# Start-up of a Fourier-mixing and gated feed-forward kernel: 128-row first stage, new transfer order, rounding on GpSimd, weight folding ahead of the activation

## The chip, the cores and the metric

One core of a Trainium2 chip. The metric is device time in microseconds (us) for one execution. Every run is compared with runs of the kernel before on the same chip in the same rounds. A ratio is the mean time of one kernel's fast runs over the mean time of the other's fast runs of the same rounds, so it is not quite the ratio of the medians that are quoted beside it.

## The reference

```python
def _attn_ref(x):                       # x: 8 x 3008 x 256, float32
    X = np.fft.fft(x, axis=1)
    X = np.fft.fft(X, axis=2)
    return X.real.astype(np.float32)

def _moe_ref(x, w_in, w_out):           # 24064 x 256, 256 x 2048, 2048 x 256
    h = x @ w_in
    g = h * (1.0 / (1.0 + np.exp(-1.702 * h)))
    return (g @ w_out).astype(np.float32)
```

## The kernel before

A sequence of 3008 is split as 94 x 32. Stage 1 is a matmul over 94 rows for each of 32 columns (folded to 16 by symmetry). A shuffle brings its result to 128 partitions, and stage 2 finishes the transform along the sequence. The transform along the 256 features is folded into the input weights (`fold_w`). Then come 384 steps of hidden layer, activation and output product. The weights arrive as 64-bit words and are rounded to float32 on the chip in eight blocks. Only the start-up differs between the two kernels: stage 1 of batch 0, the shuffle, the rounding and the weight folding of steps 1, 3 and 5.

```python
def fold_first(c):                      # a quarter of batch 0: 94-row sums and differences
    t = xt[0]
    el, eu = (hp.tile([NA, 4, D], F32, tag="h", name=n) for n in ("el", "eu"))   # NA = 94; hp has 4 buffers
    ...                                 # two small ScalarE copies and four VectorE operations a quarter; three and six in the first
def mix_first(c):
    ...
            nc.tensor.matmul(ps[:, o + c0:o + c1], lhsT=mat(w1, l0, 128), rhs=el[:, q, c0:c1], start=True, stop=False)
            nc.tensor.matmul(ps[:, o + c0:o + c1], lhsT=upper, rhs=eu[:, 3 - q, c0:c1], start=False, stop=True)

def bounds(key):                        # first half of the rounding of one weight block
    nc.scalar.activation(g[:], hi, ACTF.Square)
    nc.gpsimd.tensor_scalar(m[:], hi, scalar1=TOP, scalar2=-TOP, op0=ALU.min, op1=ALU.max)
    nc.scalar.activation(r[:].bitcast(F32), lo, ACTF.Copy, scale=2.0 ** -29, bias=2.0 ** 23)   # low word
    nc.scalar.activation(r[:], r[:].bitcast(F32), ACTF.Copy, bias=-2.0 ** 23)                   # low word
def rounded(out, key):                  # second half: three VectorE passes, then one GpSimd addition
    ...
def round_in(n):
    wst[n] = hp.tile([128, 2, 512], F32, tag="h", name="wst")
    ...
    # start of the program, cut
    warm(8); bounds(("in", 0)); round_in(0); finish_in(0)
    for c in range(4):
        fold_first(c)
        if c:
            mix_first(2 * c - 2); mix_first(2 * c - 1)
    mix_first(6); mix_first(7)
    shuffle_first(nc.sync, 0, 1); shuffle_first(nc.scalar, 2, 3); shuffle_first(nc.sync, *range(4, NG))
    load_in(2, nc.sync); fold_w(0)
    bounds(("in", 1)); round_in(1); finish_in(1)
    load_out(1, nc.sync); nyquist_weights(0); rotate(0, 0, 4, nc.scalar.copy)
    ...
    at(1, fold_w, 1); at(1, nyquist_weights, 1); at(1, rotate, 0, 4, NG)      # and 3, 5 with blocks 2, 3
    for t in range(n + LAG):
        hidden(t); product(t - LAG); activate(t); combine(t - LAG)           # bounds of t cut
        for fn, args in extra.get(t, ()): fn(*args)                          # the at(...) work
```

Of the kernel before, what the change touches and what calls it, by code (L numbers as in the profile page):

```python
# [24 lines left out]
F32 = mybir.dt.float32  # L25
# [20 lines left out]
def free(ap, offset, *dims):  # L46
    return bass.AP(ap.tensor, ap.offset + offset, [list(ap.ap[0])] + [list(d) for d in dims])


def tables(S, D):  # L50

    assert S == NA * NB and D == 256
    H = D // 2
    a, u = np.arange(NG)[:, None], np.arange(NU)[None, :]
    ks = (NG * u + a).reshape(-1)
    s = NB * np.arange(NA)[:, None, None] + np.arange(NB)[None, :, None]
    angle = 2.0 * np.pi * ((s * ks) % S) / S
    cos, sin = np.cos(angle), np.sin(angle)
    w1 = np.zeros((NA, NW + NX, NG * NU, 2))
    w1[:, 1:16, :, 0], w1[:, 1:16, :, 1] = cos[:, 1:16], sin[:, 1:16]  # L60
    w1[:, 0, :, 0], w1[:, 16, :, 1] = cos[:, 0], cos[:, 16]
    w1[:, 17, :, 0], w1[:, 18, :, 1] = sin[:, 0], sin[:, 16]
    w1[:, NW:, :, 0], w1[:, NW:, :, 1] = cos[:, :16:-1], -sin[:, :16:-1]

    j, k2 = np.arange(16)[:, None], np.arange(NB)[None, :]
    beta = 2.0 * np.pi * ((j * k2) % NB) / NB
    m2 = np.zeros((NU, 2, 16, 2, NU, NB))
    rot = np.zeros((NU, 2, 16, NU, 2, 16))
    ends = np.stack([np.ones(NB), 1.0 - 2.0 * (np.arange(NB) % 2)])
    for i in range(NU):  # L70
        m2[i, 0, :, 0, i], m2[i, 1, :, 0, i] = np.cos(beta), -np.sin(beta)
        m2[i, 0, :, 1, i], m2[i, 1, :, 1, i] = np.sin(beta), np.cos(beta)
        m2[i, :, 0, 0, i] = m2[i, :, 0, 1, i] = ends
        for n in range(16):
            rot[i, 0, n, i, 1, n], rot[i, 1, n, i, 0, n] = (1.0, -1.0) if n else (0.0, 0.0)
        rot[i, 0, 0, i, 0, 0] = rot[i, 1, 0, i, 1, 0] = 1.0

    m, d = np.arange(D)[:, None], np.arange(H)[None, :]
    phi = 2.0 * np.pi * ((m * d) % D) / D
    cd = np.stack([np.cos(phi), -np.sin(phi)], 1)  # L80
    cd[:, 1, 0] = 1.0 - 2.0 * (np.arange(D) % 2)
    cd = cd.reshape(2, H, 2, H).transpose(1, 0, 2, 3)
    small = [t.reshape(128, -1) for t in (m2, rot, cd)]
    return w1.reshape(NA, NW + NX, 96).astype(np.float32), np.concatenate(small, 1).astype(np.float32)


@with_exitstack
def kernel(ctx: ExitStack, tc, x, w_in, w_out, tab1, tab2, out):
# [20 lines left out]
    Xr = [nc.dram_tensor(f"Xr{b}", (NA, 15, D), F32, kind="Internal").ap() for b in range(B)]  # L109
    Td = [nc.dram_tensor(f"Td{b}", (NG * 128, D), F32, kind="Internal").ap() for b in range(B)]  # L110

    w1 = const.tile([NA, NW * 96 + 32], F32, tag="w1", name="w1")
    small = const.tile([128, 2 * 128 + 128 + 4 * H], F32, tag="small", name="small")
    m2 = small[:, 0:256].rearrange("p (c n) -> p c n", c=2)
    rot = small[:, 256:384]
# [5 lines left out]
    af2 = const.tile([128, NF], F32, tag="af2", name="af2")  # L121
    ones = const.tile([1, 128], F32, tag="ones", name="ones")

    def mat(w, j, n=96):
        return w[:, j * 96:j * 96 + n]

    def bank(name):
        return psm.tile([128, 512], F32, tag="mm", name=name)
# [64 lines left out]
    e4 = {}  # L193

    def load_first(c):
        t, src = xt[0], x[0].rearrange("(p j) d -> p j d", j=NB)
        for lo, hi in (((0, 4), (29, 32), (16, 17)), ((4, 8), (25, 29)), ((8, 12), (21, 25)), ((12, 16), (17, 21)))[c]:
            for p0, p1 in PIECES:
                nc.sync.dma_start(out=t[p0:p1, lo:hi, :], in_=src[p0:p1, lo:hi, :])

    def fold_first(c):

        t = xt[0]
        el, eu = (hp.tile([NA, 4, D], F32, tag="h", name=n) for n in ("el", "eu"))
        e4[c] = el, eu
        first = 29 - 4 * c
        runs = [(el, 0, 4 * c, 4, False)]
        runs += [(eu, 0, first, 4, True)] if c else [(eu, 0, first, 3, True), (eu, 3, 16, 1, False)]
        for e, i, lo, n, flip in runs:
            fwd, rev = free(t[0:NA], lo * D + 1, [D, n], [1, H - 1]), free(t[0:NA], lo * D + D - 1, [D, n], [-1, H - 1])  # L210
            nc.scalar.copy(free(e[:], i * D, [D, n], [H, 2]), free(t[0:NA], lo * D, [D, n], [H, 2]))
            nc.vector.tensor_tensor(e[:, i:i + n, 1:H], fwd, rev, op=ALU.add)
            nc.vector.tensor_tensor(e[:, i:i + n, H + 1:D], *((rev, fwd) if flip else (fwd, rev)), op=ALU.subtract)

    def mix_first(c):

        ps = bank("ps1")
        el, eu = e4[c // 2]
        for i in range(2):
            jj, o = 2 * c + i, i * D  # L220
            q = jj % 4
            ends = ((0, 16, 0, H + 1), (17, 18, H + 1, D)) if jj == 0 else ((jj, NW + jj - 1, 0, D),)
            for l0, l1, c0, c1 in ends:
                upper = mat(w1, l1, 128) if l1 < NW else mat(w1x, l1 - NW, 128)
                nc.tensor.matmul(ps[:, o + c0:o + c1], lhsT=mat(w1, l0, 128), rhs=el[:, q, c0:c1], start=True, stop=False)
                nc.tensor.matmul(ps[:, o + c0:o + c1], lhsT=upper, rhs=eu[:, 3 - q, c0:c1], start=False, stop=True)
        nc.scalar.copy(xt[0][:, 2 * c:2 * c + 2, :].rearrange("p j d -> p (j d)"), ps[0:96, :])

    def shuffle_first(eng, *part):
        if 0 not in t4t:  # L230
            t4t[0] = tp.tile([128, NG, D], F32, tag="t4", name="t4")
        for a in part:
            eng.dma_start(out=t4t[0][:, a, :], in_=xt[0][8 * a:8 * a + 8, 0:16, :])

    def warm(n):

        ps = bank("warm")
        for _ in range(n):
            nc.tensor.matmul(ps[:], lhsT=wcs[0][:, 0:128], rhs=wcs[0][:, 0:512], start=True, stop=True)
# [49 lines left out]

    pre = {}  # L290

    def bounds(key):


        hi, lo = raw[key][:, :, 1].bitcast(F32), raw[key][:, :, 0]
        g = sp.tile([128, 1024], F32, tag="s", bufs=3, name="g")
        m = cv.tile([128, 1024], F32, tag="m", name="m")
        r = cv.tile([128, 1024], U32, tag="r", bufs=2, name="r")
        nc.scalar.activation(g[:], hi, ACTF.Square)
        nc.gpsimd.tensor_scalar(m[:], hi, scalar1=TOP, scalar2=-TOP, op0=ALU.min, op1=ALU.max)  # L300

        nc.scalar.activation(r[:].bitcast(F32), lo, ACTF.Copy, scale=2.0 ** -29, bias=2.0 ** 23)
        nc.scalar.activation(r[:], r[:].bitcast(F32), ACTF.Copy, bias=-2.0 ** 23)
        pre[key] = g, m, r

    def rounded(out, key):
# [13 lines left out]
    last = {}  # L320

    def round_in(n):
        wst[n] = hp.tile([128, 2, 512], F32, tag="h", name="wst")
        last["in", n] = rounded(wst[n][:].rearrange("p i f -> p (i f)"), ("in", n))

    def round_out(n):
# [142 lines left out]

    NCK = DF // 512  # L470
    assert NCK == 4
    w1x = tp.tile([128, NG, D], F32, tag="t4", name="w1x")[0:NA].rearrange("p a d -> p (a d)")
    xt[0] = xp.tile([96, NB, D], F32, tag="x", name="xt")
    nc.vector.memset(wcs[0][:, 0:512], 1.0)
    nc.vector.memset(ones[:], 1.0)
    nc.gpsimd.memset(w1[:, NW * 96:], 0.0)
    nc.gpsimd.memset(w1x[:, NX * 96:NX * 96 + 32], 0.0)
    load_in(0, nc.sync)
    for p0, p1 in PIECES:
        nc.scalar.dma_start(out=w1[p0:p1, 0:NW * 96], in_=tab1[p0:p1, 0:NW].rearrange("p j n -> p (j n)"))  # L480
    load_first(0)
    for p0, p1 in PIECES:
        nc.scalar.dma_start(out=w1x[p0:p1, 0:NX * 96], in_=tab1[p0:p1, NW:].rearrange("p j n -> p (j n)"))
    for c in range(1, 4):
        load_first(c)
    nc.sync.dma_start(out=small[:], in_=tab2)
    load_in(1, nc.sync)
    load_out(0, nc.sync)
    warm(8)
    bounds(("in", 0))  # L490
    round_in(0)
    finish_in(0)
    for c in range(4):
        fold_first(c)
        if c:
            mix_first(2 * c - 2)
            mix_first(2 * c - 1)
    mix_first(6)
    mix_first(7)
    shuffle_first(nc.sync, 0, 1)  # L500
    shuffle_first(nc.scalar, 2, 3)
    shuffle_first(nc.sync, *range(4, NG))
    load_in(2, nc.sync)
    fold_w(0)
    bounds(("in", 1))
    round_in(1)
    finish_in(1)
    load_out(1, nc.sync)
    nyquist_weights(0)
    rotate(0, 0, 4, nc.scalar.copy)  # L510
    for cs in range(2):
        stage2(0, 0, cs)
    nyquist(0, 0)
    bounds(("out", 0))
    round_out(0)
    finish_out(0)
    load_in(3, nc.sync)

    extra = {}

    def at(t, fn, *args):
        extra.setdefault(t, []).append((fn, args))
# [2 lines left out]

    at(0, bounds, ("in", 2))
    at(0, load_out, 2, nc.sync)
    at(1, fold_w, 1)
    at(1, nyquist_weights, 1)
    at(1, rotate, 0, 4, NG)  # L530
    at(1, round_in, 2)
    at(1, bounds, ("out", 1))
    at(1, load_out, 3, nc.sync)
# [3 lines left out]
    if B > 1:  # L537
        at(2, turn, 1, 17, 32)
        at(2, load_x, 1)
    at(3, fold_w, 2)  # L540
    at(3, nyquist_weights, 2)
    at(3, finish_out, 1)
    at(3, round_in, 3)
    at(3, bounds, ("out", 2))
    at(4, finish_in, 3)
    at(4, round_out, 2)
    at(4, bounds, ("out", 3))
    at(5, fold_w, 3)
    at(5, nyquist_weights, 3)
    at(5, finish_out, 2)  # L550
    at(5, round_out, 3)
    at(6, finish_out, 3)
# [23 lines left out]
    for t in range(n + LAG):  # L576
        if t < n:
            hidden(t)
        if t == n:
            sums(n - 1)  # L580
        if t >= LAG:
            product(t - LAG)
        if t < n:
            activate(t)
        if t >= LAG:
            combine(t - LAG)
        for fn, args in extra.get(t, ()):
            fn(*args)
# [28 lines left out]
```

## Time and profile before

| | before |
|---|---|
| time, median of 3 | 2109.59 us (2109.58 to 2111.41) |
| span of the profiled run, mean granted clock | 2106.2 us, 0.982 |
| first dense stage-1 matmul / end of stage 1 | 21.5 / 49.0 us |
| first hidden matmul | 64.3 us |
| small matmuls of step 1 (`psa`) | 81.5 us |
| sums of step 8, from where TensorE sets the pace | 136.3 us |

The times in the lower rows are read from the timeline, as starts of the named instruction. The difference of such a mark between two kernels is the lead of one over the other at that point. The profile lines themselves are in the prediction below.

### The profile page before, as it was taken

To read this page: it belongs to the slowest core of one execution; us is meant where nothing else is said; L and a number is where in the kernel's file an instruction comes from. 1 tells how busy PE (TensorE), PEld (TensorE's weight loads), DVE (VectorE), ACT (ScalarE), POOL (GpSimd) and SP (SyncE) were. 2 spreads that over 40 slices of the span, in tenths; PEclk is the share of its full clock that TensorE was granted. 3 is DMA by queue.
4 is the path that set the end of the run, shared out by engine and by line. 5 is a ranking of instruction groups with operands and counts; after the bars stand their busy time and mean duration, and the time that the engine had idled before them with its cause. 6 is when DMAs were issued, how large, how long until landed. Compare 5 with 4: busy or idle time off the path is not lost.

```text
span 2106.2 us, 36069 instructions
## 1 busy us (share of the span) xinstructions
PE 2047.6 (97%) x14546; PEld 1918.2 (91%) x14546; DVE 1402.0 (67%) x2669; ACT 693.2 (33%) x978; POOL 748.6 (36%) x1035
## 2 busy tenths in 40 slices
PE   7799999999999999999999999999999999999998
PEld 5589999999999899989999999999999999999997
DVE  3557666666666666676667666767666666667676
ACT  1533333333333333333233333333333333333322
POOL 0355322442225422353224532245222542222222
PEclk6899999999999999999999999999999999999999
DMA  5631333103421143112511233220332113102100
GB/s 152 193 53 22 66 80 53 6 28 59 82 50 6 50 85 36 48 6 53 113 6 48 25 66 79 30 30 20 66 80 26 6 50 56 6 20 17 14 21 20
DMA packets 43262, 101.41 MB, mean 48 GB/s; under 512 B 4969, under 2 KB 27879, under 8 KB 41107
## 3 DMA queue, kind: packets, MB, share of 16 engines
q1 hardware_dynamic: 42575, 97.62, 24.9%
q8 instruction: 114, 1.87, 0.4%
q10 hardware_dynamic: 520, 1.49, 0.3%
q14 instruction: 53, 0.43, 0.1%
HBM read 55.83 MB, written 45.76 MB: 48 GB/s over the span
## 4 chain that ended last, share of the span: by engine, by line
PE 42%; DVE 37%; issue 10%; ACT 8%; POOL 0%; DMA 0%; ACTq 0%; DVEq 0%; SPq 0%; POOLq 0%
PE po L427 24%; DVE dif L382 8%; DVE h L384 7%; DVE h L377 7%; PE pa L370 7%; PE pb L370 6%; DVE s L401 6%; DVE s L402 6%; ACT v L376 5%; PE ps L262 1%; DVE u L454 1%; PE ps L184 1%; DVE os L454 1%; ACT xt L190 1%; PE po L415 1%
## 5 line engine op out<-in xcount | busy, mean ns | idle before, releaser
L389 ACT ACTIVATE h<-h 128x1024 f32<-128x1024 f32 x384 | 405.9, 1057 | 1337.8 <-DVE h L384 1313.9
L399 POOL TENSOR_TENSOR s<-h 128x256 f32<-128x256 f32 x376 | 273.4, 727 | 1245.6 <-issue 919.3
L377 DVE TENSOR_TENSOR h<-v,pb 128x512 f32<-128x512 f32 x384 | 263.9, 687 | 614.4 <-ACT v L376 582.8
L427 PE MATMUL po<-wt,s 128*128 128x128 f32 x4512 | 632.8, 277 | 1.1 <-DVE s L401 1.1
L427 PEld LDWEIGHTS po<-wt,s 128*128 128x128 f32 x4512 | 570.1, 193 | 1.3 <-DVE s L401 1.3
L427 PE MATMUL po<-wo,h 128*128 128x128 f32 x3008 | 463.6, 277 | 24.0 <-DVE u L454 22.9
L427 PEld LDWEIGHTS po<-wo,h 128*128 128x128 f32 x3008 | 423.5, 192 | 54.9 <-DVE u L454 36.9
L370 PE MATMUL pa<-pq,wcs 128*128 128x256 f32 x1536 | 397.1, 381 | 0.0
L370 PE MATMUL pb<-pq,wcs 128*128 128x256 f32 x1536 | 395.8, 380 | 0.0
L382 DVE SCALAR_TENSOR_TENSOR dif<-nb,af,pb 128x256 f32<-128x256 f32 x768 | 332.1, 473 | 0.0
L370 PEld LDWEIGHTS pb<-pq,wcs 128*128 128x128 f32 x1536 | 293.0, 191 | 39.7
L370 PEld LDWEIGHTS pa<-pq,wcs 128*128 128x128 f32 x1536 | 267.0, 191 | 24.4 <-issue 0.8
L384 DVE TENSOR_TENSOR h<-v,dif 128x512 f32<-128x512 f32 x384 | 279.3, 727 | 13.2
L400 POOL TENSOR_TENSOR s<-h 128x256 f32<-128x256 f32 x376 | 273.6, 728 | 0.0
L401 DVE TENSOR_TENSOR s<-s,h 128x256 f32<-128x256 f32 x376 | 241.0, 641 | 3.3 <-POOL s L399 3.3
L427 PE MATMUL po<-wo,s 128*128 128x128 f32 x1504 | 230.4, 276 | 0.0
L427 PE MATMUL po<-wt,h 128*128 128x128 f32 x1504 | 229.9, 276 | 0.0
L376 ACT COPY v<-pa 128x512 f32<-128x512 f32 x384 | 219.5, 572 | 5.0 <-PE pa L370 5.0
L402 DVE TENSOR_TENSOR s<-h,s 128x256 f32<-128x256 f32 x376 | 200.2, 532 | 12.9
L427 PEld LDWEIGHTS po<-wo,s 128*128 128x128 f32 x1504 | 199.1, 193 | 0.0
L427 PEld LDWEIGHTS po<-wt,h 128*128 128x128 f32 x1504 | 198.8, 193 | 0.0
L172 POOL TENSOR_TENSOR xt<-xt 94x510 f32<-94x510 f32 (+1 forms) x56 | 73.7, 1316 | 4.4
(73 smaller groups left out, 808.5 us busy)
## 6 DMA issues: line engine op xcount, KB each, us to landing
out_dram<-os SPq DMA_DIRECT2D x176, 128.0 KB
Td<-xt SPq DMA_DIRECT2D x7, 1536.0 KB
t<-Td SPq DMA_DIRECT2D x7, 1536.0 KB
Xr<-in_x_dram SPq DMA_DIRECT2D x7, 1410.0 KB
xt<-in_x_dram SPq DMA_DIRECT2D x7, 1280.0 KB
xt<-Xr SPq DMA_DIRECT2D x7, 1200.0 KB
nb<-pq SPq DMA_DIRECT2D x23, 256.0 KB
raw<-in_moe_w_in_dram SPq DMA_DIRECT2D x4, 1024.0 KB
```

What stands on the lines that cost most here:

```text
L172: eng.tensor_tensor(low, low, free(t, up + D - 1, [-D, n], [-1, D - 1]), op=ALU.add)
L370: nc.tensor.matmul(ps[:, i * 256:(i + 1) * 256], lhsT=wcs[cs][:, f * 128:(f + 1) * 128], rhs=pq[:, cs, ks], start=True, stop=True)
L376: nc.scalar.copy(v[:], pa[:])
L377: nc.vector.tensor_tensor(h[:, 0].rearrange("p f k -> p (f k)"), v[:], pb[:], op=ALU.add)
L382: nc.vector.scalar_tensor_tensor(dif[:, c], nb[:, ks], af2[:, f:f + 1], pb[:, c], op0=ALU.mult, op1=ALU.subtract)
L384: nc.vector.tensor_tensor(free(h[:], 512 + NB - 1, [NB, 16], [-1, NB]), v[:].rearrange("p (a k) -> p a k", k=NB), dif[:].rearrange("p (a k ...
L389: nc.scalar.activation(ht[t][:], ht[t][:], ACTF.Gelu_apprx_sigmoid)
L399: nc.gpsimd.tensor_tensor(s1, a21, a22, op=ALU.add)
L400: nc.gpsimd.tensor_tensor(s3, a11, a21, op=ALU.subtract)
L401: nc.vector.tensor_tensor(s2, s1, a11, op=ALU.subtract)
L402: nc.vector.tensor_tensor(s4, a12, s2, op=ALU.subtract)
L427: nc.tensor.matmul(pot[n][:, i, q, :], lhsT=lhs[:, q * 128:(q + 1) * 128], rhs=rhs, start=(p == 0 and i == 0 and q == 0), stop=(p == NP - ...
```

## The change

Its intent: let TensorE run the first stage at full clock by feeding it 128 rows (34 of them zeros), load the first data in fewer and better ordered transfers, take rounding work from ScalarE at the start, and let the folded weights not wait behind an activation. The core of the diff:

```diff
-    w1 = np.zeros((NA, NW + NX, NG * NU, 2))
+    w1 = np.zeros((128, NW + NX, NG * NU, 2))          # rows 94.. stay zero
+    def room_first(c):
+        e4[c] = [hp.tile([128, 4, D], F32, tag="h", name=n) for n in ("el", "eu")]
+        for e in e4[c]:
+            nc.gpsimd.memset(e[64:128], 0.0)
-                nc.tensor.matmul(ps[...], lhsT=mat(w1, l0, 128), rhs=el[:, q, c0:c1], ...)
+                nc.tensor.matmul(ps[...], lhsT=mat(w1, l0, 128, 128), rhs=el[:, q, c0:c1], ...)
+        if low:                                         # bounds(key, low): low word on GpSimd
+            low.tensor_scalar(r[:].bitcast(F32), lo, scalar1=2.0 ** -29, scalar2=2.0 ** 23, op0=ALU.mult, op1=ALU.add)
+            low.tensor_scalar(r[:], r[:].bitcast(F32), scalar1=-2.0 ** 23, scalar2=None, op0=ALU.add)
-        wst[n] = hp.tile([128, 2, 512], F32, tag="h", name="wst")
+        pool, tag = (hp, "h") if n else (op, "os")      # block 0 no longer takes one of four buffers
-    for p0, p1 in PIECES:
-        nc.scalar.dma_start(out=w1[p0:p1, ...], in_=tab1[p0:p1, ...])
+    nc.scalar.dma_start(out=w1[:, 0:NW * 96], in_=tab1[:, 0:NW * 96])
-    warm(8)
-    bounds(("in", 0))
+    warm(12)
+    room_first(0); room_first(1)
+    bounds(("in", 0), nc.gpsimd)                        # also for ("in", 1) and ("out", 0)
-    shuffle_first(nc.sync, 0, 1)
-    shuffle_first(nc.scalar, 2, 3)
-    shuffle_first(nc.sync, *range(4, NG))
+    shuffle_first(nc.scalar, 2, 3)
+    shuffle_first(nc.sync, 0, 1)
     load_in(2, nc.sync)
 ...
     load_out(1, nc.sync)
+    shuffle_first(nc.sync, *range(4, NG))
-    at(1, fold_w, 1); at(1, nyquist_weights, 1)         # and 3, 5
+    early[1] = 1                                        # run after product(t - LAG), before activate(t)
-    at(1, rotate, 0, 4, NG)
+    at(4, rotate, 0, 4, NG)
```

(Cut: the x transfers in fewer pieces and the indices of the tables.)

More of the change, by code (lines that the diff above doesn't have):

```diff
@@ L58, in tables @@
     cos, sin = np.cos(angle), np.sin(angle)
-    w1 = np.zeros((NA, NW + NX, NG * NU, 2))
-    w1[:, 1:16, :, 0], w1[:, 1:16, :, 1] = cos[:, 1:16], sin[:, 1:16]
-    w1[:, 0, :, 0], w1[:, 16, :, 1] = cos[:, 0], cos[:, 16]
-    w1[:, 17, :, 0], w1[:, 18, :, 1] = sin[:, 0], sin[:, 16]
-    w1[:, NW:, :, 0], w1[:, NW:, :, 1] = cos[:, :16:-1], -sin[:, :16:-1]
+    w1 = np.zeros((128, NW + NX, NG * NU, 2))
+    w1[:NA, 1:16, :, 0], w1[:NA, 1:16, :, 1] = cos[:, 1:16], sin[:, 1:16]
+    w1[:NA, 0, :, 0], w1[:NA, 16, :, 1] = cos[:, 0], cos[:, 16]
+    w1[:NA, 17, :, 0], w1[:NA, 18, :, 1] = sin[:, 0], sin[:, 16]
+    w1[:NA, NW:, :, 0], w1[:NA, NW:, :, 1] = cos[:, :16:-1], -sin[:, :16:-1]
     j, k2 = np.arange(16)[:, None], np.arange(NB)[None, :]
@@ L83, in tables @@
     small = [t.reshape(128, -1) for t in (m2, rot, cd)]
-    return w1.reshape(NA, NW + NX, 96).astype(np.float32), np.concatenate(small, 1).astype(np.float32)
+    return w1.reshape(128, -1).astype(np.float32), np.concatenate(small, 1).astype(np.float32)
 @with_exitstack
@@ L110 @@
     Td = [nc.dram_tensor(f"Td{b}", (NG * 128, D), F32, kind="Internal").ap() for b in range(B)]
-    w1 = const.tile([NA, NW * 96 + 32], F32, tag="w1", name="w1")
+    w1 = const.tile([128, NW * 96 + 32], F32, tag="w1", name="w1")
     small = const.tile([128, 2 * 128 + 128 + 4 * H], F32, tag="small", name="small")
@@ L122, with mat @@
     ones = const.tile([1, 128], F32, tag="ones", name="ones")
-    def mat(w, j, n=96):
-        return w[:, j * 96:j * 96 + n]
+    def mat(w, j, rows=NA, n=96):
+        return w[0:rows, j * 96:j * 96 + n]
     def bank(name):
@@ L195, in load_first @@
     def load_first(c):
-        t, src = xt[0], x[0].rearrange("(p j) d -> p j d", j=NB)
-        for lo, hi in (((0, 4), (29, 32), (16, 17)), ((4, 8), (25, 29)), ((8, 12), (21, 25)), ((12, 16), (17, 21)))[c]:
-            for p0, p1 in PIECES:
-                nc.sync.dma_start(out=t[p0:p1, lo:hi, :], in_=src[p0:p1, lo:hi, :])
+        for p0, p1 in PIECES:
+            t, src = xt[0][p0:p1], x[0].rearrange("(p j) d -> p j d", j=NB)[p0:p1]
+            if c:
+                both = [(29 - 8 * c) * D, 2], [1, 4 * D]
+                nc.sync.dma_start(out=free(t, 4 * c * D, *both), in_=free(src, 4 * c * D, *both))
+                continue
+            for lo, hi in ((0, 4), (29, 32), (16, 17)):
+                nc.sync.dma_start(out=t[:, lo:hi, :], in_=src[:, lo:hi, :])
+    def room_first(c):
+        e4[c] = [hp.tile([128, 4, D], F32, tag="h", name=n) for n in ("el", "eu")]
+        for e in e4[c]:
+            nc.gpsimd.memset(e[64:128], 0.0)
     def fold_first(c):
         t = xt[0]
-        el, eu = (hp.tile([NA, 4, D], F32, tag="h", name=n) for n in ("el", "eu"))
-        e4[c] = el, eu
+        el, eu = e4[c]
         first = 29 - 4 * c
@@ L209, in fold_first @@
         for e, i, lo, n, flip in runs:
+            e = e[0:NA]
             fwd, rev = free(t[0:NA], lo * D + 1, [D, n], [1, H - 1]), free(t[0:NA], lo * D + D - 1, [D, n], [-1, H - 1])
-            nc.scalar.copy(free(e[:], i * D, [D, n], [H, 2]), free(t[0:NA], lo * D, [D, n], [H, 2]))
+            nc.scalar.copy(free(e, i * D, [D, n], [H, 2]), free(t[0:NA], lo * D, [D, n], [H, 2]))
             nc.vector.tensor_tensor(e[:, i:i + n, 1:H], fwd, rev, op=ALU.add)
@@ L223, in mix_first @@
             for l0, l1, c0, c1 in ends:
-                upper = mat(w1, l1, 128) if l1 < NW else mat(w1x, l1 - NW, 128)
-                nc.tensor.matmul(ps[:, o + c0:o + c1], lhsT=mat(w1, l0, 128), rhs=el[:, q, c0:c1], start=True, stop=False)
+                upper = mat(w1, l1, 128, 128) if l1 < NW else mat(w1x, l1 - NW, 128, 128)
+                nc.tensor.matmul(ps[:, o + c0:o + c1], lhsT=mat(w1, l0, 128, 128), rhs=el[:, q, c0:c1], start=True, stop=False)
                 nc.tensor.matmul(ps[:, o + c0:o + c1], lhsT=upper, rhs=eu[:, 3 - q, c0:c1], start=False, stop=True)
@@ L290, with bounds @@
     pre = {}
-    def bounds(key):
+    def bounds(key, low=None):
         hi, lo = raw[key][:, :, 1].bitcast(F32), raw[key][:, :, 0]
@@ L300, in bounds @@
         nc.gpsimd.tensor_scalar(m[:], hi, scalar1=TOP, scalar2=-TOP, op0=ALU.min, op1=ALU.max)
-        nc.scalar.activation(r[:].bitcast(F32), lo, ACTF.Copy, scale=2.0 ** -29, bias=2.0 ** 23)
-        nc.scalar.activation(r[:], r[:].bitcast(F32), ACTF.Copy, bias=-2.0 ** 23)
+        if low:
+            low.tensor_scalar(r[:].bitcast(F32), lo, scalar1=2.0 ** -29, scalar2=2.0 ** 23, op0=ALU.mult, op1=ALU.add)
+            low.tensor_scalar(r[:], r[:].bitcast(F32), scalar1=-2.0 ** 23, scalar2=None, op0=ALU.add)
+        else:
+            nc.scalar.activation(r[:].bitcast(F32), lo, ACTF.Copy, scale=2.0 ** -29, bias=2.0 ** 23)
+            nc.scalar.activation(r[:], r[:].bitcast(F32), ACTF.Copy, bias=-2.0 ** 23)
         pre[key] = g, m, r
@@ L322, in round_in @@
     def round_in(n):
-        wst[n] = hp.tile([128, 2, 512], F32, tag="h", name="wst")
+        pool, tag = (hp, "h") if n else (op, "os")
+        wst[n] = pool.tile([128, 2, 512], F32, tag=tag, name="wst")
         last["in", n] = rounded(wst[n][:].rearrange("p i f -> p (i f)"), ("in", n))
@@ L471 @@
     assert NCK == 4
-    w1x = tp.tile([128, NG, D], F32, tag="t4", name="w1x")[0:NA].rearrange("p a d -> p (a d)")
+    w1x = tp.tile([128, NG, D], F32, tag="t4", name="w1x")[:].rearrange("p a d -> p (a d)")
     xt[0] = xp.tile([96, NB, D], F32, tag="x", name="xt")
@@ L478 @@
     load_in(0, nc.sync)
-    for p0, p1 in PIECES:
-        nc.scalar.dma_start(out=w1[p0:p1, 0:NW * 96], in_=tab1[p0:p1, 0:NW].rearrange("p j n -> p (j n)"))
-    load_first(0)
-    for p0, p1 in PIECES:
-        nc.scalar.dma_start(out=w1x[p0:p1, 0:NX * 96], in_=tab1[p0:p1, NW:].rearrange("p j n -> p (j n)"))
-    for c in range(1, 4):
+    nc.scalar.dma_start(out=w1[:, 0:NW * 96], in_=tab1[:, 0:NW * 96])
+    nc.scalar.dma_start(out=w1x[:, 0:NX * 96], in_=tab1[:, NW * 96:])
+    for c in range(4):
         load_first(c)
@@ L488 @@
     load_out(0, nc.sync)
-    warm(8)
-    bounds(("in", 0))
+    warm(12)
+    room_first(0)
+    room_first(1)
+    bounds(("in", 0), nc.gpsimd)
     round_in(0)
@@ L497 @@
             mix_first(2 * c - 1)
+            if c + 1 < 4:
+                room_first(c + 1)
     mix_first(6)
     mix_first(7)
+    shuffle_first(nc.scalar, 2, 3)
     shuffle_first(nc.sync, 0, 1)
-    shuffle_first(nc.scalar, 2, 3)
-    shuffle_first(nc.sync, *range(4, NG))
     load_in(2, nc.sync)
     fold_w(0)
-    bounds(("in", 1))
+    bounds(("in", 1), nc.gpsimd)
     round_in(1)
@@ L513 @@
     nyquist(0, 0)
-    bounds(("out", 0))
+    bounds(("out", 0), nc.gpsimd)
     round_out(0)
@@ L517 @@
     load_in(3, nc.sync)
-    extra = {}
+    extra, early = {}, {}
     def at(t, fn, *args):
@@ L527 @@
     at(0, load_out, 2, nc.sync)
-    at(1, fold_w, 1)
-    at(1, nyquist_weights, 1)
-    at(1, rotate, 0, 4, NG)
+    early[1] = 1
     at(1, round_in, 2)
@@ L539 @@
         at(2, load_x, 1)
-    at(3, fold_w, 2)
-    at(3, nyquist_weights, 2)
+    early[3] = 2
     at(3, finish_out, 1)
@@ L547 @@
     at(4, bounds, ("out", 3))
-    at(5, fold_w, 3)
-    at(5, nyquist_weights, 3)
+    early[5] = 3
     at(5, finish_out, 2)
@@ L582 @@
             product(t - LAG)
+        if t in early:
+            fold_w(early[t])
+            nyquist_weights(early[t])
         if t < n:
```

## The prediction

> **What bounds the kernel now.** I read the page first: busy shares and the 40 slices.
>
> ```profile
> PE 2047.6 (97%) x14546; PEld 1918.2 (91%) x14546; DVE 1402.0 (67%) x2669; ACT 693.2 (33%) x978; POOL 748.6 (36%) x1035
> PE   7799999999999999999999999999999999999998
> PEclk6899999999999999999999999999999999999999
> ```
>
> TensorE is full from slice 3 on, at full clock; a slice is 52.7 us. Only the first two slices (about 105 us) have gaps and a low clock, and the diff touches nothing later than step 6 of 384. So the change can shorten only the start-up, and an upper bound is what TensorE loses there. I then cut the start into windows (columns: stretch, length, busy us of PE, PEld, DVE, ACT, POOL, granted clock, DMA share, GB/s).
>
> ```profile
> 20.00:40.00 20.00, 18.50 (x46) 14.36 (x47) 7.70 (x15) 2.74 (x8) 1.10 (x1) 0.50 0.59 185
> 60.00:80.00 20.00, 11.27 (x40) 6.97 (x39) 8.34 (x11) 11.95 (x14) 6.03 (x4) 0.84 0.78 233
> 120.00:140.00 20.00, 20.00 (x90) 17.45 (x89) 7.95 (x14) 6.06 (x8) 11.04 (x15) 0.91 0.00 1
> ```
>
> From 20 to 40 us TensorE is busy nearly all the time but at clock 0.50; from 60 to 80 us it waits half the time; from 120 us on it is full. Next the timeline, in order of time, for the reason (start, length, what, idle before it and its releaser).
>
> ```profile
> 20.14 0.54 DVE L212 TENSOR_TENSOR eu<-xt 94x381 f32<-94x381 f32 x1
> 21.50 0.77 PE L226 MATMUL ps<-eu,w 94*128 94x129 f32 x2 [3.15 <-DVE eu L212]
> ...
> 48.12 1.06 PE L226 MATMUL ps<-eu,w1x 94*128 94x256 f32 x2
> ...
> 48.97 5.01 PE L347 MATMUL psw<-wst,small 128*128 128x512 f32 x8
> ...
> 52.10 0.19 PEld L347 LDWEIGHTS psw<-wst,small 128*128 128x128 f32 x1 [0.24 <-issue]
> ```
>
> The first stage of batch 0 (94-row matmuls) runs back to back from 21.5 to 49.2 us and never leaves half clock in 27 us; the 128-row weight folding that follows is at full clock about 3 us after it starts (weight loads 0.85 us apart, then 0.43). The chain of waits between 49 and 120 us shows what comes then:
>
> ```profile
> 50.63 6.27 DMA t<-xt
> 56.90 1.81 issue
> ...
> 72.41 1.06 ACT h L389
> 73.47 1.11 ACT g L299
> 74.58 1.02 ACT r L302
> 75.62 1.06 ACT r L303
> ...
> 80.47 0.97 ACT wcs L348 x2
> 81.48 1.86 PE psa L353 x8
> ```
>
> A shuffle transfer, then ScalarE: activation, three rounding passes, and only behind them the copies of the folded weights, on which TensorE waits. The same pattern returns at 102 and 116 us. After about 121 us TensorE sets the pace and a gain made before is kept.
>
> **What the Trainium skill says.** "TensorE: Matmul & The Clock Gate", Part 1: TensorE idles at half clock and is released after one busy window of about 3.4 us, and falls back after an idle one. The trace agrees for 128 rows (warming matmuls from 1.46 to about 7.4 us cold, then fast; the clock falls again at about 14.9 us, some 3.6 us after they end), but 27 us of dense 94-row work was not released; the page says nothing of rows. That rows are what counts is my inference. "SBUF — State Buffer", the section with the single rule on contention: a VectorE instruction with two SBUF inputs contends with a GpSimd one that reads SBUF, not with one that only writes; the loser blocks for the whole instruction. The trace agrees: a fold subtraction of 0.67 us took 2.82 us (17.40 to 20.22) while GpSimd's 2.64 us addition ran. So the new zero-fills should not block the folds, but the new rounding passes on GpSimd can block VectorE's rounding. "DMA: Bandwidth & Descriptors", Queues, rings and completion order: the queues of SyncE and ScalarE use the same 16 engines and alternate[...].
>
> **The change part by part.**
>
> *128 rows.* A chunk of the first stage is 8 units of a 256-column matmul; a unit takes 0.853 us cold (1.06 lines are 0.853 apart), so 4 chunks take 27.3 us, and 13.7 us at full clock. Start: raw weights land at 12.4 us as before. VectorE's three rounding passes were 13.66 to 16.9 us; two new GpSimd passes (about 1.1 us each, from the 1.13 us of GpSimd's clamp of the same shape) begin as the clamp ends at 13.6 and contend: I allow 2 us of delay. The table grows from 1.2 to 1.67 MB, at about 245 KB per us 2 us more, but x's first chunk (about 16.5 us) still lands before VectorE is free. So dense matmuls start at about 23.5 instead of 21.5 us. They run cold for about 4.5 us (5.3 units), then 2.7 units at 0.43: chunk 0 ends at about 29.2. Chunk 1 is folded by then, because the old first buffer, the rounded weights, no longer takes one of the four buffers: ends 32.6. Chunks 2 and 3 need a zero-fill (estimate under 1 us) and a fold (8 VectorE pieces of 0.6 us per two chunks, 2.4 us each) between release and use: about 3.6 us against 3.4 of matmul. All x has landed by about 26 us (5.75 MB), so data do not bound. End of the stage: 29.2 + 3.4 + 2 x 3.6 = 39.8 us against 49.2 + 0.1: about 9.4 us saved.
>
> *Shuffle order.* Before, the first four slices shared the queues with eight more: 8.9 us from the last copy at 49.8 to the first use at 58.7. Now the eight come after two weight loads. I expect about 7 us: 1.9 saved. The eight slices are needed only at step 4, long after.
>
> *Two rounding passes on GpSimd* for three of eight blocks: 2.2 us less on ScalarE each. At 54.5 us they lie beside the shuffle and are free; in the third block ScalarE's copy v waits behind them, but VectorE's rounding of that block (g at 64.97, h at 69.23) sets the step, so nothing is saved but a few tenths. First hidden matmul: 64.28 - 9.4 - 1.9 = about 53 us. GpSimd then has clamp, two passes and addition (1.1 x 3 + 2.4 = 5.7 us) per block in some 10 us: it holds, with little to spare.
>
> *Folding before the activation.* Step 1: the weight copies run at 77.2 instead of 80.4 us, and 0.4 us of rotation leaves the place: 3.2 us earlier for step 2's matmuls, though ScalarE's own chain gains only about 2.0 (activation now behind the small matmuls). Step 3: about nothing gained on ScalarE, since copies wait for the folding matmuls themselves and the activation is now behind them (1.06 us given back), but the lead of 2 to 3 us stays. Step 5: weights, small matmuls and copies come directly behind the folding, which saves the rest of the 116.0 to 117.8 gap and with it the slow stretch that follows (16 matmul passes in 4.57 instead of 3.45 us, and pb 1.44 instead of 0.86). Walking both chains to the product of step 4 (121.4 us before) gives 5 to 6 us; I take 5.9.
>
> Sum: 9.4 + 1.9 + 5.9 = 17.2 us. 2109.6 - 17.2 = 2092.4 us; I say 2092.
>
> **The rivals.**
>
> 1. *Rows are not what holds the clock.* Then the first stage stays cold, 27.3 us, and pays the 2 us of contention: saved 1.9 + 5.9 - 2 = 6 us, time about 2104. For it: the page ties the gate to busy time alone, and zero rows do no useful work. Against it: 27 us of dense 94-row work at 0.50, and release by the next 128-row work in 3 us. I give it 15%.
> 2. *GpSimd becomes the wait.* Clamp, two passes, zero-fills and addition run in one queue; if an integer pass costs like the integer addition (2.4 us) instead of 1.1, each of the three blocks takes 2.6 us more; the first delays the folds, the third the first activation: 4 to 5 us lost, time about 2097. For it: the addition's 2.4 us, and the 2.82 us fold. Against it: the passes are of the one-input kind, like the clamp.
> 3. *The start is bound by x.* With later issue behind larger tables, chunk 3 could land after 30 us. The transfer queue gave about 250 GB/s until 31 us, with later weights in it; for 5.75 MB that is 25 to 26 us. It would cost 2 to 4 us.
> 4. *The gain is given back later*: GpSimd's differences and the next batch's folds set the end at 143 to 152 us. GpSimd stood idle 8.7 us before step 8's sums, so an earlier start finds room; and the next batch's loads are issued in the same chain, so they move with it. At most 2 or 3 us.
>
> **Range and chances.** Central 2092. With rival 1 2104, with 2 and 3 together about 2099; if contention is absent and the clock is released in one window, 20 us or a little more are saved: 2087. Range 2084 to 2103. Faster by 2% would need 41 us, more than the 29 us that TensorE's low clock and about 25 us of idle could give only together and in full: 1%. Slower by 2% has no mechanism: 1%. Within 2%: 98%.
>
> **What would show it right or wrong.** In the windows of the changed kernel: clock near 1.0 from about 28 us on in the 20 to 40 us stretch (right), or 0.50 throughout (rival 1). First hidden matmul at about 53 us. VectorE's first rounding passes ending near 19 instead of 16.9 us. GpSimd's new passes at about 1.1 us each (rival 2: 2 us or more). In the first 125 us the folding copies come ahead of the activation and TensorE's wait before the small matmuls of step 1 is shorter by about 3 us. From step 8 on, step by step, the same durations shifted by some 17 us; if the shift at 121 us is larger than the total's gain, something was given back later. The prediction is wrong if the total leaves 2084 to 2103, or if the shift sits elsewhere than in these three parts.

## The result, and the profile after

The changed kernel took 2092.89 us (median of 4, 2092.26 to 2093.24) against 2109.59 us (median of 4); the ratio is 0.9921, 95% interval 0.9904 to 0.9939. The prediction was 2092 us. A later control run with five rounds gave 0.9924. The change is real and smaller than 2%.

The page of the changed kernel, busy shares and the slices, which answer to the first lines of the prediction:

```profile
PE 2034.2 (97%) x14554; PEld 1907.5 (91%) x14554; DVE 1404.5 (67%) x2669; ACT 687.5 (33%) x972; POOL 771.6 (37%) x1049
PE   7899999999999999999999999999999999999998
PEclk8999999999999999999999999999999999999999
```

Only the first slices differ. The windows of the start (columns as in the prediction: stretch, length, busy PE, PEld, DVE, ACT, POOL, clock, DMA share, GB/s):

```profile
20.00:40.00 20.00, 16.99 (x68) 14.39 (x69) 11.01 (x16) 5.29 (x12) 10.06 (x8) 0.83 0.52 159
60.00:80.00 20.00, 13.61 (x48) 10.02 (x47) 12.67 (x18) 11.81 (x15) 7.28 (x4) 0.83 0.50 174
120.00:140.00 20.00, 19.93 (x131) 18.28 (x130) 10.62 (x18) 6.14 (x11) 13.93 (x21) 1.00 0.21 7
```

Between 20 and 40 us the clock is 0.83 instead of 0.50 and TensorE issues 68 matmul passes instead of 46. The chain of waits of the changed kernel names where the release happens and what came after:

```profile
25.93 0.85 PE ps L236 x2
26.78 0.45 PE ps L235 x2
27.23 0.43 PE ps L236 x2
...
41.03 8.69 DMA t<-xt
...
67.02 1.06 ACT r L317
68.07 0.47 ACT v L391
68.55 0.98 ACT wcs L363 x2
69.58 1.86 PE psa L368 x8
```

A unit (the two passes of one 256-column matmul) goes from 0.85 to 0.43 us at about 26.7 us, 4.9 us after the dense matmuls begin. The shuffle's piece of the chain is 8.69 us; before, it was 6.27 us of transfer and 1.81 us that the profile puts down to nothing, 8.08 us in all. In step 1 the weight copies (`wcs`) stand directly behind `v`; in the kernel before an activation and more stood between.

The lead over the kernel before at the marks, with the experiments told below (differences of starts in the profiled runs; the last row is the difference of spans):

| mark (before, us) | changed | rows94 | late_fold | passes_act | combo_warm |
|---|---|---|---|---|---|
| first dense stage-1 matmul (21.50) | -0.2 | 0.4 | 0.3 | 1.9 | 1.8 |
| end of stage 1 (48.97) | 9.6 | 0.8 | 9.8 | 12.7 | 15.0 |
| first hidden matmul (64.28) | 8.5 | -1.4 | 8.6 | 11.2 | 15.9 |
| small matmuls of step 1 (81.48) | 11.9 | 2.0 | 8.7 | 14.6 | 19.2 |
| sums of step 8 (136.31) | 15.9 | 6.1 | 10.9 | 18.4 | 25.6 |
| end (2106.2) | 16.1 | 6.5 | 11.1 | 18.0 | 25.6 |

The lead at step 8 is the lead at the end to within 0.4 us in every column: what is won before TensorE sets the pace is kept. A yardstick for the other differences: the control run below is the changed kernel profiled again, and its leads are 10.8 us at the end of stage 1 (its clock was released 3.0 us after the dense start, against 4.9), 8.7 at the first hidden matmul and 15.5 at step 8. So a mark can differ by about 1 us between two profiles of one kernel.

### The profile page after: what moved, and what is told of

It reads as the page before. It is cut to its first block, busy times and chain, and to the rows that moved or that the text cites. A ratio compares the mean times of both kernels' runs of the same rounds, so it can differ in the third digit from the quotient of the medians.

```text
span 2090.1 us, 36077 instructions
## 1 busy us (share of the span) xinstructions
PE 2034.2 (97%) x14554; PEld 1907.5 (91%) x14554; DVE 1404.5 (67%) x2669; ACT 687.5 (33%) x972; POOL 771.6 (37%) x1049
## 4 chain that ended last, share of the span: by engine, by line
PE 44%; DVE 36%; issue 10%; ACT 8%; DMA 1%; POOL 1%; ACTq 0%; DVEq 0%; SPq 0%; POOLq 0%
PE po L442 25%; DVE dif L397 8%; PE pa L385 7%; DVE h L399 7%; DVE h L392 7%; PE pb L385 7%; DVE s L417 6%; DVE s L416 6%; ACT v L391 5%; PE ps L272 1%; DVE u L469 1%; PE po L430 1%; PE ps L184 1%; ACT xt L190 1%; DVE os L469 1%
```

## The experiments

Twelve kernels ran, all with correct results.

**rows94: the matmuls on 94 rows again, all else as changed.**

```diff
-    lhsT=mat(w1, l0, 128, 128), rhs=el[:, q, c0:c1]
+    lhsT=mat(w1, l0, 94, 128), rhs=el[0:94, q, c0:c1]          # the same for upper and eu
```

> The changed kernel, but the first stage's matmuls read rows 0 to 94 again; zero-fills, buffers, order and rounding stay. Theory A (the number of rows decides whether the clock is released): clock 0.50 from about 22 us to the end of the stage, each 256-column unit 0.853 us, the stage ends at about 49 us instead of 39.4, total about 2102 (9 to 10 us above the changed kernel). Rival (the clock rose because of the longer warm-up, the fourth buffer or the earlier data, not the rows): clock released at about 26 us as in the changed kernel, stage ends at about 39 us, total 2093.

Measured: 2101.29 us, ratio 0.9969 (0.9952 to 0.9985). Its window from 20 to 40 us:

```profile
20.00:40.00 20.00, 18.89 (x47) 15.26 (x48) 10.34 (x16) 3.54 (x9) 7.65 (x7) 0.50 0.49 154
```

The clock stays at 0.50 and the stage ends at 48.1 us. Zero-fills, longer warm-up and the extra buffer are all there, so none of them releases the clock: the rows do. This is worth 8.8 us at the end of the stage (10.0 against the control's profile) and about 9 us in the total: 8.4 by the medians, 9.6 by the spans.

**rows95, rows96, rows97: where is the limit?** The same edit with 95, 96 and 97, one profiled run each.

> The same with rows 0 to 97, one row more than three groups of 32. If what counts is how many groups of 32 rows an instruction touches, the clock is released as with 128 rows (stage ends near 39 us). If what counts is the number of rows in proportion, 97 is hardly more than 94 and the clock stays at 0.50 (stage ends near 49 us).

> The changed kernel with matmuls over rows 0 to 96, exactly three groups of 32. With 94 rows the clock stayed at 0.50 and with 97 it was released. If the fourth group of 32 decides, 96 stays at 0.50 as 94 did and the total is about 2101; if the limit is anywhere between 94 and 96 rows, it is released and the total is about 2093.

> The changed kernel with matmuls over rows 0 to 95. 94 rows left the clock at 0.50, 96 and 97 released it, so the theory of a fourth group of 32 has fallen; 96 is three quarters of 128. If the limit is three quarters of the rows, 95 stays at 0.50 from 22 us to the end of the stage (near 48 to 49 us), total about 2101. If it lies between 94 and 95, or if 94 is special in another way, it is released and the total is about 2092.

Measured: 97 rows 2092.69 us, 96 rows 2092.04 us, 95 rows 2102.3 us (unknown state, single runs). The window of 95 rows, then that of 96:

```profile
20.00:40.00 20.00, 18.68 (x47) 15.12 (x48) 10.55 (x16) 3.54 (x9) 7.53 (x8) 0.50 0.52 159
```

```profile
20.00:40.00 20.00, 17.46 (x68) 14.71 (x69) 10.54 (x16) 5.28 (x12) 9.60 (x8) 0.82 0.51 157
```

After 97 rows I held that a matmul must touch the fourth group of 32 rows. The 96-row run brought that down: three groups suffice if they are full. The limit lies between 95 and 96 of 128 rows. Whether it is "three quarters of the rows" or "three full groups" these runs cannot tell apart. So 128 rows were more than needed; two zero rows would have done.

**rows_alone: the kernel before with the 128 rows only** (tables and fold buffers of 128 rows, zero-fills, tables in one transfer each; cut):

```diff
-        el, eu = (hp.tile([NA, 4, D], F32, tag="h", name=n) for n in ("el", "eu"))
-        e4[c] = el, eu
+        if c:
+            room_first(c)
+        el, eu = e4[c]                  # room_first(0) stands before bounds(("in", 0))
```

> The kernel before with nothing changed but the rows: tables and fold buffers of 128 rows with zeros, matmuls over all of them, the tables in one transfer each. If the rows carry the first term by themselves, the clock is released about 4 us into the stage, the stage ends at 38 to 42 us instead of 49, the lead stays to the end, and the total is 7 to 10 us below the kernel before. If the fourth buffer is needed too (the old rounding still holds one, so chunk 1's second half is zeroed and folded only after chunk 0), TensorE waits between chunks and the gain is 4 to 7 us.

Measured: 2103.0 us, ratio 0.9977 (0.996 to 0.9994), about 5 us. The stage ends at 41.9 us: 7.1 us of lead instead of 9.6, although this kernel starts its dense matmuls 2.1 us earlier than the changed one. Its timeline at the end of chunk 0 shows the wait:

```profile
24.90 0.59 PE L232 MATMUL ps<-el,w 128*128 128x256 f32 x2
25.64 0.95 POOL L204 MEMSET el<- 64x1024 f32 x1
25.72 0.68 DVE L219 TENSOR_TENSOR eu<-xt 94x508 f32<-94x508 f32 x1 [4.80 <-POOL eu L204]
27.15 0.67 PE L233 MATMUL ps<-eu,w1x 128*128 128x256 f32 x2 [1.66 <-DVE eu L220]
```

The second half of chunk 1 is zeroed and folded only after chunk 0 has been read, and TensorE waits 1.66 us; the same wait returns at each chunk (1.66 and 2.56 us). So the fast clock needs the fourth buffer to pay in full, as the second branch of the expectation had it. The kernel before folds as late, but at half clock that hid nearly all of it: at 28.9 us its weight loads stood idle 0.51 us, and its matmuls lost about 0.15 us a chunk. (The fourth buffer was not taken out alone; the claim rests on this wait and on the changed kernel, where one wait of 1.27 us is left.)

**late_fold: folding and rotation back at their old places.**

```diff
-    early[1] = 1                        # 3 and 5 likewise
-    at(4, rotate, 0, 4, NG)
+    at(1, fold_w, 1)
+    at(1, nyquist_weights, 1)
+    at(1, rotate, 0, 4, NG)
```

> The changed kernel with the weight folding of steps 1, 3 and 5 behind the activation and the rotation in step 1, as before. My theory: this part is worth 7.4 us (the lead grew from 8.5 us at the first hidden matmul to 15.9 us at step 7), so the total is about 2100 and TensorE's wait before the small matmuls of step 1 is about 3 us longer. Rival (most of the 7.4 us came from the earlier start or from rounding on GpSimd): under 3 us, total below 2096.

Measured: 2097.45 us, ratio 0.9953 (0.9938 to 0.9967), against 0.9924 for the control of the next batch: about 6 us by the ratios, 5.0 us by the spans (2095.1 and 2090.1). That is less than the 7.4 us expected and more than the rival's 3. The chain of waits in step 1:

```profile
67.95 0.48 ACT v L391
...
70.69 1.06 ACT h L404
71.74 0.97 ACT wcs L363 x2
72.75 1.86 PE psa L368 x8
```

The small matmuls come at 72.75 instead of 69.58 us, 3.2 us later, with the same start (60.6 and 60.7 us for the first step's sum): exactly what stands between `v` and `wcs`, VectorE's pieces (cut above) and the activation. The rest of the 7.4 us that the lead grew after the first hidden matmul (2.3 us) is in this kernel as well, between step 1 and step 8, so it can be had without the folding: rows_alone, with the folding late and no rounding moved to GpSimd, gains the same 2.3 us there (5.3 to 7.7). But it does not need the earlier start either: rows94, with the folding ahead and its first hidden matmul 1.4 us later than before, gains the whole 7.5 us. So the folding is worth 5.0 us in a kernel that starts early, and the 2.3 us come with either change. One dip of the clock makes 1.7 of them: in the kernel before it falls once more from 120.1 to 123.5 us, and there `pb` takes 1.44 us and sixteen passes of `po` 4.57, against 0.86 and 3.45. late_fold and rows_alone have the same wait of 1.5 us in front of step 5's small matmuls, just before that point, and no dip. Why the clock falls in one and not in the others is not shown.

**passes_act: the low-word passes back on ScalarE.**

```diff
-    bounds(("in", 0), nc.gpsimd)        # and ("in", 1), ("out", 0)
+    bounds(("in", 0))
```

> The changed kernel with the two low-word rounding passes of all three blocks back on ScalarE. My theory now: on GpSimd they are worth nothing and cost about 1.9 us, since in the second block they hold the shared read port while VectorE folds chunk 3 (its two eu pieces 1.62 and 1.60 us instead of 0.68); without them the stage ends about 1.9 us earlier and the total is 2091 or a little less. Rival (they relieve ScalarE on the path): total 2095 or more, with the first hidden step later by 2 us.

Measured: 2089.35 us, ratio 0.9914 (0.9899 to 0.9929): by the spans 1.9 us faster than the changed kernel (2088.2 and 2090.1), and 2.4 us ahead at step 8; by the ratios, across batches, 0.1% with overlapping intervals. The direction rests on the trace, where the cause is plain. Changed kernel, the end of chunk 3's fold:

```profile
32.73 1.33 POOL L310 TENSOR_SCALAR m<-raw 128x1024 f32<-128x1024 f32 x1
32.98 1.62 DVE L222 TENSOR_TENSOR eu<-xt 94x508 f32<-94x508 f32 x1
34.13 1.45 POOL L313 TENSOR_SCALAR r<-raw 128x1024 f32<-128x1024 uint32 x1
34.52 1.60 DVE L223 TENSOR_TENSOR eu<-xt 94x508 f32<-94x508 f32 x1
36.27 0.67 PE L236 MATMUL ps<-eu,w1x 128*128 128x256 f32 x2 [1.27 <-DVE eu L223]
```

Both fold pieces end about 0.5 us after a GpSimd pass ends; alone they take 0.68 us. In passes_act the clamp (`m`) still blocks the first, the second is 0.67 us again, and TensorE's wait is 0.34 instead of 1.27 us:

```profile
30.57 1.33 POOL L310 TENSOR_SCALAR m<-raw 128x1024 f32<-128x1024 f32 x1
30.82 1.62 DVE L222 TENSOR_TENSOR eu<-xt 94x508 f32<-94x508 f32 x1
32.37 0.67 DVE L223 TENSOR_TENSOR eu<-xt 94x508 f32<-94x508 f32 x1
33.19 0.67 PE L236 MATMUL ps<-eu,w1x 128*128 128x256 f32 x2 [0.34 <-DVE eu L223]
```

The first block is the larger part: dense matmuls begin at 19.6 instead of 21.7 us, since VectorE's three rounding passes no longer share their reads with GpSimd (3.2 against 4.7 us from the first one's start to the last one's end), and the first data landed 0.6 us earlier in that run. The rounding on GpSimd is a part of the change that works against it.

**control, old_shuffle, load2_early: what does the order of the shuffle do?** Five rounds each, on one chip. old_shuffle puts the eight later slices back directly behind the first four; load2_early issues the third input-weight load before the first stage:

```diff
     finish_in(0)
+    load_in(2, nc.sync)                 # load2_early; removed from its place between the slices
     for c in range(4):
```

> The changed kernel itself, as a yardstick on this chip for the runs beside it. Ratio to the kernel before 0.992, time 2091 to 2093, first hidden matmul at about 55.8 us.

> The changed kernel with the order of the shuffle before: all twelve slices together, then the two weight loads. My prediction said the new order saves 1.9 us; the trace of the changed kernel shows 9.6 us from the first issue to the first use, against 8.9 before. Theory now (the two megabyte loads on the same queue take what the eight deferred slices gave): with the old order the first use comes about 9 us after the first issue, and the total is 0 to 1 us below the control. If the new order does save time under the new timing, the first use comes at 11 us or later and the total is 1 to 2 us above.

> The changed kernel with the third input-weight load issued right behind the rounding of the first block (at about 17 us, into the transfer queue that is idle from 34 to 40 us) instead of between the shuffle slices. If that load's bandwidth is what stretches the first four slices, they are used about 6 to 7 us after their first issue instead of 9.6, and the total falls 2 to 3 us below the control. If the slices are slow by themselves (1 KB pieces over 128 rows, issue cost), the gap stays above 9 us and the total is that of the control.

| | time | ratio (95%) | first slice issued to first use |
|---|---|---|---|
| control | 2092.88 | 0.9924 (0.9911 to 0.9936) | 9.7 us |
| old_shuffle | 2093.43 | 0.9928 (0.9916 to 0.9941) | 9.3 us |
| load2_early | 2092.7 | 0.9924 (0.9912 to 0.9937) | 10.1 us |

Neither order nor the megabyte load changes the time beyond the intervals. These are wide (about 2.6 us each way), but the runs side by side are not: their means are 2092.6, 2093.6 and 2092.7 us. So the new order can be worth about 1 us at most, and not through the first four slices, which take 9 to 10 us in all three and were quickest in the old order. (In the profiled run of old_shuffle, its slowest, the third block's data landed late and held ScalarE 1.53 us; the median does not show it.) The windows of load2_early in which nothing but the first four slices moves:

```profile
40.00:42.00 2.00, 1.91 (x5) 0.57 (x3) 0.00 (x0) 0.64 (x2) 0.00 (x0) 1.00 0.34 38
42.00:44.00 2.00, 1.05 (x8) 0.96 (x8) 0.34 (x1) 1.73 (x3) 0.00 (x0) 1.00 0.45 69
```

The slices alone get 38 to 69 GB/s at a DMA share under one half. So they are slow before anything else moves. A possible reason is in the Trainium skill, "DMA: Bandwidth & Descriptors", the section on why a DMA increments its semaphore by 16: a transfer is spread over the largest number up to 16 that divides both slowest dimensions, and a slice has 8 source rows, so 8 of 16 engines. A share of 0.45 agrees with it, and so does the trace's record of single packets: of the slices' 1 KB packets never more than 8 are in flight from 40 to 42.9 us. Whether a shape over 16 engines would be faster stays open; no run here changed it.

**combo and combo_warm: a version that beats both.** combo has the early load, all passes on ScalarE and `warm(18)`. combo_warm adds five warming matmuls in each of two waits:

```diff
+    warm(5)                             # before the first rotate
+            if t == 1:                  # between fold_w and nyquist_weights of step 1
+                spare = pso.tile([128, 512], F32, tag="o3", name="spare")
+                for _ in range(5):
+                    nc.tensor.matmul(spare[:], lhsT=wcs[0][:, 0:128], rhs=wcs[0][:, 0:512], start=True, stop=True)
```

> A version meant to beat both: the early load, all rounding passes back on ScalarE, 18 warming matmuls instead of 12 so that TensorE is still at full clock when the first stage begins, and 5 warming matmuls each in the shuffle's wait and in the wait before the small matmuls of step 1. Estimate from the traces: 2.4 us (passes) + 2 us (first chunk at full clock) + 1.5 us (second stage at full clock) + 2.5 us (steps 1 and 2 at full clock) + 0 to 3 us (load), so 8 to 11 us below the control, 2082 to 2085. If the clock does not stay up in these waits, it is about 2 to 5 us below.

> The combined version without the two groups of 5 warming matmuls in the waits of the shuffle and of step 1 (early load, passes on ScalarE, 18 warming matmuls at the start kept). Estimate: those groups are worth 1.5 us in the second stage and about 2.5 us in steps 1 and 2, so this is about 4 us slower than the version with them: 2087. If the passes and the hot start carry everything, it is equal, 2083.

Measured: combo 2088.16 us, ratio 0.9905 (0.9891 to 0.992); combo_warm 2083.37 us, ratio 0.9883 (0.9868 to 0.9898), 9.5 us faster than the control beside it. The two differ by about 4.8 us by the medians (4.6 by the ratios, 5.1 by the spans), where 4 were expected. The windows of combo_warm:

```profile
20.00:40.00 20.00, 18.99 (x84) 14.55 (x83) 8.72 (x13) 8.42 (x16) 5.00 (x5) 1.00 0.71 218
40.00:60.00 20.00, 17.86 (x61) 9.73 (x60) 8.65 (x10) 11.62 (x16) 7.35 (x4) 1.00 0.63 161
60.00:80.00 20.00, 18.24 (x80) 13.62 (x79) 15.02 (x20) 13.89 (x19) 7.13 (x4) 1.00 0.74 243
```

The clock never leaves 1.00 from 20 us on. Dense matmuls start hot at 19.7 us and stage 1 ends at 34.0 us, 2.3 us before passes_act. The sixteen stage-2 passes take 2.03 us, against 3.76 in combo, and the first matmuls of step 2 run hot (`pa` 1.13 us instead of 2.08). This agrees with the rule on idle time in the Trainium skill, "TensorE: Matmul & The Clock Gate", "Why this matters for your kernels": no idle gaps of more than about 3 us between bursts of matmuls. In combo TensorE waited 5.4 us in each of the two places and the clock fell; in combo_warm none of its waits from 34 to 75 us is over 1.1 us.

## Why the prediction was right

The total was right: 2092 predicted, 2092.9 measured, 17.2 us of gain against 16.7 by the medians and 16.1 by the spans. That is partly luck, since two of its three terms erred in opposite directions.

1. *128 rows release the clock* (9.4 us predicted for the stage, 9.6 measured): right, and rows94 shows that the rows are the cause (8.8 us of it). The inference that "rows are what counts" holds, but with a limit between 95 and 96. Within the term two sizes were off and cancelled. The contention at the start was put at 2 us; VectorE's passes lost 1.5 us, and the first block landed 1.2 us earlier (clamp at 11.24 instead of 12.48 us), so the dense start moved by 0.2 us only, and VectorE's passes ended at 17.1 us and not near 19. rows_alone, whose only transfer change is the tables in one piece, has the earlier landing too. In exchange GpSimd held up the fold of chunk 3, which the prediction did not have. One reading in its working is off: the clock fell at 14.3 us after the warming matmuls, 2.7 us after their end at 11.55, not at 14.9 and 3.6.
2. *Shuffle order saves 1.9 us*: wrong, the step that failed. The wait from the first slice's issue to its use grew from 8.9 to 9.7 us, and the first hidden matmul came at 55.8 us, not at about 53. The step assumed that the eight later slices took bandwidth from the first four; the three shuffle runs show 9.3 to 10.1 us whatever stands behind them.
3. *Folding ahead of the activation, 5.9 us*: the lead grew by 7.4 us there. late_fold puts 5.0 us (by spans) on the folding itself, near the walk; step 1 gained 3.2 us, as worked out. The other 2.3 us are in late_fold and rows_alone too, without the folding. 1.7 of them are the dip of the clock at 120 us; the walk had counted it as saved by the folding, but it is gone from these two kernels as well.
4. *GpSimd passes at about 1.1 us each*: wrong in size for the second one. In the third block, where VectorE's rounding did not overlap them, they took 1.11 and 2.77 us. Rival 2 had named just this and put the loss at 4 to 5 us; passes_act shows 1.9 to 2.4 us. "At 54.5 us they lie beside the shuffle and are free" was wrong for the second block: moved to GpSimd, they ran at 34 us, beside the folds.
5. *Rivals 1, 3 and 4*: rival 1 fell with rows94 (its 2104 us is what that kernel nearly shows, 2101.3). Rival 3 did not show: TensorE's waits between chunks end on folds, not on data. Rival 4 neither: the lead at step 8 is the lead at the end.

## What to carry to other kernels

When TensorE is dense and yet at half clock, look at how many of the 128 rows its matmuls use before looking for gaps: here two more rows of zeros, 96 instead of 94, took a stage from 27.0 to 18.1 us. Once the matmuls run at full clock, waits that they had hidden appear (buffers, folds, shared reads), so take out those in the same change and check each part alone; one part here, the rounding on GpSimd, cost time. Where a short wait cannot be removed, a few idle matmuls in it keep the clock for what follows.

## What the Trainium skill lacked or had wrong

- "TensorE: Matmul & The Clock Gate", Part 1, ties the release of the clock to a busy window of about 3.4 us and says nothing of rows. Here 27 us of dense matmuls on 94 rows, and likewise the whole stage on 95, stayed at 0.50, while 96, 97 and 128 rows were released 3 to 6 us after the dense matmuls began.
- "SBUF — State Buffer", the section with the single rule, was right on what contends: GpSimd zero-fills (0.95 us) left the folds at 0.68 us, GpSimd passes that read stretched them to 1.6 us. But that the loser blocks for the whole instruction did not hold for one pair of the first block, alike in the nine profiles that have it: GpSimd's second pass ran from 14.69 to 17.79 us and VectorE's third, begun later, from 15.19 to 17.13. It ended first, and both took longer than without the other (3.10 against 2.77 us, 1.94 against 1.23), as far as the profiler's spans on GpSimd, which are rough, can be trusted.
- I found no page with the cost of a GpSimd scalar pass by output type: 128x1024 took 1.11 us from 32-bit integer to float and 2.77 us from float to 32-bit integer.
- "DMA: Bandwidth & Descriptors" gives the split over engines but no rate for slices of 8 source rows onto 128 partitions: 128 KB slices in 1 KB pieces moved at 38 to 69 GB/s in all, at a DMA share of 0.34 to 0.45 (windows of load2_early).
